# Last stages of a spectral mixer as 64- and 32-row matmul tiles, eight per product

## The chip, the cores and the metric

The kernel runs on one core of one Trainium2 chip. The metric is the device time of one execution in microseconds (us). TensorE (PE) multiplies matrices and loads weights (PEld); VectorE (DVE), ScalarE (ACT) and GpSimd (POOL) compute elementwise; DMAs are issued from the queues of SyncE (SP), ACT and POOL. Results of PE lie in PSUM, eight banks; everything else on the chip lies in SBUF.

## What is computed

With x of shape (1, 2048, 640), the kernel mixes two long convolutions with a gate per row:

```
g = sigmoid((x * gate_w).sum(-1, keepdims=True))
# a: K[d, l] = 2 Re sum_n C[d, n] exp(A[d, n] dt[d] l);
#    y = irfft(rfft(x^T, 4096) * rfft(K, 4096))[:2048];  a = y^T + x * D_skip
# b: irfft2(rfft2(x) * (w_r + i w_i))
out = g * a + (1 - g) * b
```

## The kernel before

Everything is 32-bit floating point. The transforms of length 4096 are done in stages, each a set of small matmuls. Columns (640 of them) are handled as four blocks c of 160. Rows are l = 64 b + a with b below 32 and a below 64.

- `phase_a`, first half: `stage1` (L328) and `stage2` (L340) transform x and store it to DRAM as u_d; at its end four copies (L441) put the gate sums of the rows into `T.gate`, 16 columns of 128 partitions.
- `phase_a`, second half: the part b. `front` loads a slice (ue, L475; ww, L478), `channels`, `filt`, `back1` transform and filter, and `back2` (L559) does the inverse and stores each 128-row result s3 to DRAM as s3e_d by one DMA (L570, L572), from SP for the first six slices, from POOL for the last three.
- `phase_p` and `phase_b`, merged with it: the kernel K of the convolution; y (L679, L680) on POOL feeds the matmuls p_k (L693).
- `phase_c` and `phase_d`: the transform of K in `first`, and block by block the product with u_d and the way back. This last stage is where the change lies.

`phase_d` handles, for each block c, five groups of pairs of frequencies. `fronts` (L784) loads us, does `stage2` into PSUM (p_s2, L348), and on DVE and POOL the complex product (ma, mb, t2; L795 to L801). `backs` (L804) multiplies by `T.w3` into PSUM (p_i2, L814), copies to s3 on ACT (L816, L818), and ACT's queue stores s3 to DRAM as s3_d (L823, and L820 for the single last pair, whose rows overwrite rows of group 8's store). `load_c` (L856) reads s3_d back as t3, with frequency on the partitions, by SP (once by ACT); `load_e` (L852) reads s3e_d as t3e. The last stages then are:

- `last_e` (L868): pieces of three, three and two columns a; `halved` (L157) multiplies t3e by `T.e3e` as two tiles of 128 rows and 64 columns; DVE multiplies by 1 - g into oe (L876).
- `last_c` (L881): the same pieces, from t3 with `T.e3`, two tiles of 128 rows and 64 columns (L893); DVE multiplies by g into ot (L898) and POOL adds oe (L899). For the last block DVE does both in one instruction per column (L896), 16 in all. Output rows go out by DMA (L901, L904, L954).

`T.e3` and `T.e3e` hold the 32-column matrix of the last step in blocks with zeros elsewhere, so that one matmul of 128 rows does two (or four) blocks of the contraction. Each 32-bit matmul shows as two records in the trace, each with a weight load.

PSUM in `phase_d`: the pool `c_ps` of three tiles of two banks for p_s1, p_s2 and p_i2, and the pool `d_ps` of two tiles of one bank for the last stages. A new tile waits until the tile that had its place has been read.

The order of the work: `merge` (L163) draws from several generators by the costs that they yield and their weights. In each group, `mains` (fronts of this group, backs of one or more groups before), `last_e` or `last_c` for the block before, and two steps of `first` for the next block go side by side. `last_e` of block c runs beside groups 1 and 2 (2 and 3 for c = 0), `last_c` of block c - 1 beside groups 3 and 4 for c = 1 and 2. `last_c` of blocks 2 and 3 comes at the end. `behind` only keeps an order on one engine. The engines are strict queues: what stands behind a waiting instruction waits too.

Of the kernel before, what the change touches and what calls it, by code (L numbers as in the profile page):

```python
# [9 lines left out]
F32 = mybir.dt.float32  # L10
# [40 lines left out]
def _tables():  # L51
# [14 lines left out]
    e3 = np.zeros((64, 2, 2, 32))  # L66
    for j in range(2):
        e3[:, j, j, :] = kr

    e3e = np.zeros((32, 4, 4, 32))  # L70
    for r in range(4):
        e3e[:, r, JR[r], :] = kr[32:64]
    one = np.tile(np.eye(32), (4, 1))
    c1 = np.concatenate([
        e1[0], e1[1], e3.reshape(4, 32, 64).swapaxes(0, 1).reshape(128, 64), e3e.reshape(128, 128), np.eye(128), one,
# [16 lines left out]
    w3 = np.swapaxes(w3, 0, 1).reshape(128, NP * 128)  # L92
# [37 lines left out]
    return {"t_c1": f(c1), "t_w2": f(w2), "t_w3": f(w3), "t_td": f(td),  # L130
# [17 lines left out]
def _lay_back(y):  # L148
    y = y.reshape(4, 2, 2, 32, 16, 160)
    return np.ascontiguousarray(y.transpose(3, 2, 1, 4, 0, 5).reshape(1, L, D))  # L150
# [4 lines left out]


def halved(nc, out, w, x):  # L157

    for i in (0, 64):
        nc.tensor.matmul(out[i:i + 64], w[:, i:i + 64], x, start=True, stop=True)  # L160
# [23 lines left out]
def body(tc, A, out):  # L184
    nc = tc.nc
    T = Ctx()
    with ExitStack() as top:
        dram = top.enter_context(tc.tile_pool(name="dram", bufs=1, space=DRAM))
        T.u_d = dram.tile([4, 128, 17, 2, 160], F32, name="u_d")
        T.s3e_d = dram.tile([4, 32, 64, 160], F32, name="s3e_d")  # L190
        T.s3_d = dram.tile([4, 64, 64, 160], F32, name="s3_d")
# [12 lines left out]

        T.e1 = [take(128), take(128)]
        T.e3, T.e3e, T.id, T.one = take(64), take(128), take(128), take(32)
# [146 lines left out]
def phase_a(tc, A, T):  # L353
# [3 lines left out]
    with ExitStack() as ctx:  # L357
# [82 lines left out]
        for r, x in enumerate((slice(31, 15, -1), slice(32, 48), slice(15, None, -1), slice(48, 64))):  # L440
            V.tensor_copy(T.gate[32 * r:32 * r + 32, 0, :], p[32 * r:32 * r + 32, x])  # L441


    with ExitStack() as ctx:
# [16 lines left out]
        w3v = A["t_w3"].rearrange("p (k m) -> p k m", m=128)  # L461
# [8 lines left out]
        def front(pr, st):  # L470
            nl = st.nl = 128 if pr < 8 else 64
            st.w3 = w3p.tile([128, 2, 128], F32, tag="w3", name="w3")
            nc.sync.dma_start(st.w3[:, 0:nl // 64, :], w3v[:, 16 + 2 * pr:16 + 2 * pr + nl // 64, :])
# [85 lines left out]
        def back2(st, pr, j):  # L559
# [9 lines left out]
            if kk < 16:  # L569
                dma(T.s3e_d[:, 2 * kk:2 * kk + 2].rearrange("c k a d -> (k a) c d"), s3.rearrange("p (c d) -> p c d", c=4))  # L570
            else:
                dma(T.s3e_d[:, 1].rearrange("c a d -> a c d"), s3[0:64].rearrange("p (c d) -> p c d", c=4))  # L572
# [193 lines left out]
def phase_d(tc, A, T, ctx, out):  # L766
# [9 lines left out]
    ps = ctx.enter_context(tc.tile_pool(name="c_ps", reuse_waits="tile", bufs=3, space=PSUM))  # L776
    pd = ctx.enter_context(tc.tile_pool(name="d_ps", reuse_waits="tile", bufs=2, space=PSUM))
# [26 lines left out]
    def backs(c, g0, gn, st):  # L804
# [4 lines left out]
        for h in range(0, np_, 4):  # L809
# [9 lines left out]
            if k0 == 32:  # L819
                nc.scalar.dma_start(T.s3_d[c, 33], s3[0:64, 0, :])  # L820
            elif h or (c, g0) == (3, 12):
                x = h if (c, g0) == (3, 12) else 0
                T.sd = nc.scalar.dma_start(T.s3_d[c, 2 * (k0 + x):2 * (k0 + h) + 8].rearrange("(x k) a d -> (k a) x d", k=2), s3[:, x:h + 4, :])  # L823
# [16 lines left out]
    def gate(i, a, n):  # L840
        return T.gate[:, i, a:a + n].unsqueeze(2).broadcast_to([128, n, 160])
# [10 lines left out]
    def load_e(c):  # L852
        t3es[c] = dk.tile([128, 16, 160], F32, tag="t3e", name="t3e")
        nc.sync.dma_start(t3es[c][:, :, :], T.s3e_d[c].rearrange("k (r a) d -> (k r) a d", r=4))

    def load_c(c, p, n, parts=1, eng=nc.sync):  # L856
# [5 lines left out]
        w = 16 // parts  # L862
        for y in range(p // 16, (p + n) // 16):
            src = T.s3_d[c, 16 * y:16 * y + 16].rearrange("k (j x a) d -> (k j) x a d", x=2, j=2)
            for a in range(0, 16, w):
                T.ld = eng.dma_start(t3s[c][y::4, :, a:a + w], src[:, :, a:a + w])

    def last_e(c, a):  # L868

        oe = oes[c, a] = o4.tile([128, AG, 160], F32, tag="oe", name="oe")  # L870
        for i in range(0, AG, 3):
            n = min(3, AG - i)
            p = pd.tile([128, 3, 160], F32, tag="pd", name="p_e")
            with behind(T.mm):
                halved(nc, p[:, 0:n], T.e3e, t3es[c][:, a + i:a + i + n])
            V.tensor_tensor(out=oe[:, i:i + n], in0=p[:, 0:n], in1=gate(1, a + i, n), op=ALU.mult)  # L876
            yield 0.8
# [3 lines left out]
    def last_c(c, a):  # L881
# [6 lines left out]
        for i in range(0, AG, 3):  # L888
            n = min(3, AG - i)
            p = pd.tile([128, 3, 160], F32, tag="pd", name="p_c")  # L890
            with behind(T.mm):
                for x in range(2):
                    P.matmul(p[64 * x:64 * x + 64, 0:n], T.e3, t3[:, x, a + i:a + i + n], start=True, stop=True)  # L893
            if c == 3:
                for j in range(n):
                    V.scalar_tensor_tensor(out=ot[:, i + j], in0=p[:, j], scalar=T.gate[:, 0, a + i + j:a + i + j + 1], in1=oe[:, i + j], op0=ALU.mult, op1=ALU.add)  # L896
            else:
                V.tensor_tensor(out=ot[:, i:i + n], in0=p[:, 0:n], in1=gate(0, a + i, n), op=ALU.mult)  # L898
                (V if c == 2 and a and n < 3 else G).tensor_tensor(out=ot[:, i:i + n], in0=ot[:, i:i + n], in1=oe[:, i:i + n], op=ALU.add)  # L899
            if c < 2 and i + n == AG:  # L900
                G.dma_start(out[c, :, a:a + AG], ot[:, :, :])  # L901
            elif c == 3 and i + n > (5 if a else 6):
                x = i if a and i > 3 else 0
                nc.sync.dma_start(out[c, :, a + x:a + i + n], ot[:, x:i + n])  # L904
            yield 0.8
# [72 lines left out]
```

## Time and profile before

| | |
|---|---|
| time, median of 3 runs | 609.3 us |
| lowest and highest | 607.72 and 2746.93 us |
| the profiled execution: its time | 608.74 us |
| its span in the profile | 607.0 us |
| mean granted TensorE clock | 0.966 |
| HBM | 60.91 MB read, 39.98 MB written |

The median stands 0.6 us above the profiled execution. In rows of instruction groups, "out<-in" names the tile written and those read (buffer numbers left out; a tile goes by a shortened name, so t3 appears as t, s3_d as s_d, e3 as c), and "128*64 128x480" is a matmul on 128 rows and 64 columns of the array, over 480 elements. "idle before <-releaser" is how long the engine sat idle and what ended it.

### The profile page before, as it was taken

To read this page: it belongs to the slowest core of one execution; us is meant where nothing else is said; L and a number is where in the kernel's file an instruction comes from. 1 tells how busy PE (TensorE), PEld (TensorE's weight loads), DVE (VectorE), ACT (ScalarE), POOL (GpSimd) and SP (SyncE) were. 2 spreads that over 40 slices of the span, in tenths; PEclk is the share of its full clock that TensorE was granted. 3 is DMA by queue.
4 is the path that set the end of the run, shared out by engine and by line. 5 is a ranking of instruction groups with operands and counts; after the bars stand their busy time and mean duration, and the time that the engine had idled before them with its cause. 6 is when DMAs were issued, how large, how long until landed. Compare 5 with 4: busy or idle time off the path is not lost.

```text
span 607.0 us, 16654 instructions
## 1 busy us (share of the span) xinstructions
PE 535.8 (88%) x7084; PEld 405.6 (67%) x7084; DVE 500.2 (82%) x748; ACT 364.8 (60%) x659; POOL 267.0 (44%) x246
## 2 busy tenths in 40 slices
PE   9688979989968989989798999898989999999874
PEld 7576657766656657676566676565878877787631
DVE  5971597598899989999999899979399796987974
ACT  4556775576846876888589888799723332231210
POOL 4931252053525344454326335416254347547441
PEclk9899989989989996998899999999999999999998
DMA  8787204245612320332250233006685989889776
GB/s 341 293 288 268 79 5 151 69 154 181 239 43 67 97 87 13 108 118 109 67 151 12 75 97 110 24 28 200 224 346 184 356 273 299 291 271 310 225 231 239
DMA packets 48083, 101.98 MB, mean 168 GB/s; under 512 B 3316, under 2 KB 32776, under 8 KB 46248
## 3 DMA queue, kind: packets, MB, share of 16 engines
q1 hardware_dynamic: 24888, 67.74, 32.3%
q10 hardware_dynamic: 20080, 22.52, 11.9%
q0 software_dynamic: 3040, 10.65, 5.3%
q8 instruction: 56, 0.92, 0.6%
q14 instruction: 19, 0.16, 0.1%
HBM read 60.91 MB, written 39.98 MB: 166 GB/s over the span
## 4 chain that ended last, share of the span: by engine, by line
PE 51%; DVE 27%; ACT 9%; DMA 8%; issue 4%; POOL 1%; ACTq 0%; DVEq 0%; POOLq 0%; SPq 0%
PE p_eo L551 8%; PE p_s L348 8%; PE p_s L335 6%; PE p_e L638 5%; PE p_k L693 4%; PE p_i L814 4%; PE p_p L649 3%; DVE q L652 3%; PE p_d L518 2%; DVE t L801 2%; PE p_i L565 2%; PE p_t L502 2%; DVE ma L795 2%; PE p_c L893 2%; PE p_d L519 2%
## 5 line engine op out<-in xcount | busy, mean ns | idle before, releaser
L679 POOL TENSOR_TENSOR y<-e,sc 128x512 f32<-128x512 f32 x40 | 56.7, 1418 | 131.0 <-ACT sc L665 60.3
L348 PE MATMUL p_s<-t,w 128*64 128x160 f32 x1056 | 92.4, 314 | 10.2 <-ACT ut L382 5.1
L348 PEld LDWEIGHTS p_s<-t,w 128*64 128x64 f32 x1056 | 76.5, 139 | 21.4 <-ACT ut L382 6.0
L640 ACT ACTIVATE e<-p_e 128x512 f32<-128x512 f32 x120 | 68.6, 602 | 22.7 <-PE p_e L638 20.4
L551 PE MATMUL p_eo<-td,pmt 107*128 107x321 f32 x204 | 69.0, 459 | 3.9 <-ACT pmt L505 3.9
L693 PE MATMUL p_k<-x,y 128*32 128x64 f32 x2560 | 63.6, 229 | 9.8 <-DVE x L677 2.9
L693 PEld LDWEIGHTS p_k<-x,y 128*32 128x32 f32 x2560 | 46.1, 113 | 38.0 <-issue 29.4
L652 DVE SCALAR_TENSOR_TENSOR q<-q,p_p 128x512 f32<-128x512 f32 x80 | 53.4, 681 | 13.5 <-ACT q L651 11.8
L336 ACT COPY t<-p_s 128x512 f32<-128x512 f32 x40 | 24.6, 623 | 65.2 <-PE p_s L335 41.8
L638 PE MATMUL p_e<-rm,par 128*128 128x512 f32 x120 | 58.7, 519 | 3.4 <-ACT e L640 2.8
L680 POOL TENSOR_TENSOR y<-e,sc 128x512 f32<-128x512 f32 x40 | 54.5, 1362 | 6.5 <-ACT sc L666 6.5
L800 POOL TENSOR_TENSOR t<-ma 64x320 f32<-64x320 f32 x32 | 28.0, 875 | 61.4 <-DVE ma L795 51.8
L551 PEld LDWEIGHTS p_eo<-td,pmt 107*128 107x128 f32 x204 | 38.4, 198 | 19.6 <-ACT pmt L505 6.9
L677 DVE TENSOR_TENSOR x<-e,cx 128x1024 f32<-128x1024 f32 x40 | 48.6, 1214 | 2.2 <-ACT cx L668 2.2
L651 ACT ACTIVATE q<-p_p 128x512 f32<-128x512 f32 x80 | 46.5, 592 | 4.2 <-PE p_p L649 3.8
L649 PE MATMUL p_p<-rp,par 128*128 128x512 f32 x80 | 43.5, 548 | 4.5 <-DVE q L652 4.5
L814 PE MATMUL p_i<-t,w 128*64 128x160 f32 x528 | 42.7, 300 | 4.4 <-POOL t L801 3.4
L335 PE MATMUL p_s<-c,kt 128*64 128x128 f32 x640 | 43.0, 274 | 3.9 <-DVE mb L796 2.0
L335 PEld LDWEIGHTS p_s<-c,kt 128*64 128x64 f32 x640 | 38.0, 136 | 12.6 <-issue 7.7
L816 ACT COPY s<-p_i 128x640 f32<-128x640 f32 x32 | 21.8, 694 | 40.0 <-PE p_i L814 30.4
L335 PE MATMUL p_s<-c,u 128*64 128x128 f32 x640 | 41.5, 278 | 2.5 <-ACT ut L382 2.5
L795 DVE TENSOR_TENSOR ma<-p_s,us 128x640 f32<-128x640 f32 (+1 forms) x36 | 28.2, 784 | 18.8 <-PE p_s L348 11.5
(153 smaller groups left out, 1181.5 us busy)
## 6 DMA issues: line engine op xcount, KB each, us to landing
u_d<-ut SPq DMA_DIRECT2D x32, 320.0 KB, 2.6
us<-u_d ACTq DMA_DIRECT2D x16, 640.0 KB, 6.0
s_d<-s ACTq DMA_DIRECT2D x15, 640.0 KB, 8.3
t<-s_d SPq DMA_DIRECT2D x14, 640.0 KB, 5.9
ww<-in_w_l SPq DMA_DIRECT2D x8, 642.0 KB, 4.0
ue<-u_d SPq DMA_DIRECT2D x8, 640.0 KB, 4.4
k_d<-kt SPq DMA_DIRECT2D x4, 1280.0 KB, 7.6
kt<-k_d SPq DMA_DIRECT2D x8, 640.0 KB, 5.9
```

The lines of the kernel that those rows point to most:

```text
L335: nc.tensor.matmul(p[64 * ri:64 * ri + 64, j, :], src(i + j), e1[ri], start=True, stop=True)
L348: ins = nc.tensor.matmul(p[64 * j:64 * j + 64, i, 160 * ri:160 * ri + 160], w2[:, x, 64 * ri:64 * ri + 64], t1[:, x // 2 if x < 32 else K0 ...
L551: P.matmul(p[:, :E], st.pmt[:DC, c, w, j, :], tv[:DC, w, c, :], start=c == 0, stop=c == 2)
L638: P.matmul(p[:, :], pars[t], rm[:, c:c + 512], start=True, stop=True)
L640: st.exp = S.activation(ef[:, c:c + 512], p[:, :], AF.Exp)
L649: P.matmul(p[:, :], pars[t], rp[:, c:c + 512], start=True, stop=True)
L652: V.scalar_tensor_tensor(out=qf[:, c:c + 512], in0=qf[:, c:c + 512], scalar=MAGIC, in1=p[:, :], op0=ALU.subtract, op1=ALU.subtract)
L677: V.tensor_tensor(out=x[:, 0].rearrange("p d (h j) -> p d h j", h=2), in0=e[:, :, 0:64].rearrange("p d (h j) -> p d h j", h=2), in1=cx.uns ...
L679: G.tensor_tensor(out=y[:, 1], in0=e[:, :, 64:96], in1=sc[:, 0], op=ALU.mult)
L680: G.tensor_tensor(out=y[:, 0], in0=e[:, :, 64:96], in1=sc[:, 1], op=ALU.mult)
L693: P.matmul(st.pb[32 * r:32 * r + 32, o, :], y[:, ri, 4 * qq + JR[r], :], x[:, ri, 4 * qq + JR[r], :], start=t % 2 + qq + 1 - ri == 0, stop ...
L814: T.mm = P.matmul(p[x:x + 64, i // 2, 160 * (i % 2):160 * (i % 2) + 160], T.w3[:, k0 + h + i, x:x + 64], t2[:, h + i, :], start=True, stop ...
```

## The change

The last stages do a product in eight matmuls: four blocks s of output partitions (32 columns each) times two halves j of the contraction rows. For `last_c` each matmul has 64 rows, for `last_e` 32, and each covers two columns a (320 elements). One product thus gives four columns, in two PSUM banks, one for each j; a group of eight columns is two products instead of three pieces. `T.e3` and `T.e3e` lose their zeros and shrink to 32 columns. The products share the pool `c_ps`, now four tiles of two banks; `d_ps` is gone.

To have the rows in the order that this needs, the columns of `T.w3` are permuted (and a second table `t_w3e` serves part b), s3_d and s3e_d have new shapes, each store of s3_d goes out as two DMAs over every second partition, and each store of s3e_d as four over every fourth. Loads of t3 that were cut in two by columns are cut by the halves x. The gate is written by 16 copies instead of four, and the output's row order changes with it. The core of the diff:

```
-        for r, x in enumerate((slice(31, 15, -1), slice(32, 48), slice(15, None, -1), slice(48, 64))):
-            V.tensor_copy(T.gate[32 * r:32 * r + 32, 0, :], p[32 * r:32 * r + 32, x])
+        for r in range(4):
+            o = slice(32 * r, 32 * r + 32)
+            g = T.gate[o, 0, :].rearrange("p (x j v) -> p x j v", x=2, j=2)
+            for x in range(2):
+                i = 16 * x + 4 * r
+                V.tensor_copy(g[:, x, 0], p[o, 31 - i:(27 - i if i < 28 else None):-1])
+                V.tensor_copy(g[:, x, 1], p[o, 32 + i:36 + i])
...
-            if kk < 16:
-                dma(T.s3e_d[:, 2 * kk:2 * kk + 2].rearrange("c k a d -> (k a) c d"), s3.rearrange("p (c d) -> p c d", c=4))
+            sv = s3.rearrange("p (c d) -> p c d", c=4)
+            for r in range(4):
+                if kk < 16:
+                    dma(T.s3e_d[:, r, 2 * kk:2 * kk + 2].rearrange("c k a d -> (k a) c d"), sv[r::4])
...
-    ps = ctx.enter_context(tc.tile_pool(name="c_ps", reuse_waits="tile", bufs=3, space=PSUM))
-    pd = ctx.enter_context(tc.tile_pool(name="d_ps", reuse_waits="tile", bufs=2, space=PSUM))
+    ps = ctx.enter_context(tc.tile_pool(name="c_ps", reuse_waits="tile", bufs=4, space=PSUM))
...
+            for j in range(2):
+                if k0 == 32:
+                    nc.scalar.dma_start(T.s3_d[c, 2, j, 1], s3[j:64:2, 0, :])
+                elif h or (c, g0) == (3, 12):
+                    x = h if (c, g0) == (3, 12) else 0
+                    T.sd = nc.scalar.dma_start(T.s3_d[c, g0 // 4, j, 2 * x:2 * h + 8].rearrange("(x k) a d -> (k a) x d", k=2), s3[j::2, x:h + 4, :])
...
+    def product(w, t, x, v, rows):
+
+        p = ps.tile([128, 2, 512], F32, tag="ps", name="p_l")
+        with behind(T.mm):
+            for s in range(4):
+                for j in range(2):
+                    r = slice(64 * j + rows[0], 64 * j + rows[1])
+                    P.matmul(p[32 * s:32 * s + 32, j, 0:320], w[r, :], t[r, 4 * s + v:4 * s + v + 2, :], start=True, stop=True)
+        return p[:, :, 0:320].rearrange("p j (v d) -> p j v d", v=2)
...
-        for i in range(0, AG, 3):
-            n = min(3, AG - i)
-            p = pd.tile([128, 3, 160], F32, tag="pd", name="p_e")
-            with behind(T.mm):
-                halved(nc, p[:, 0:n], T.e3e, t3es[c][:, a + i:a + i + n])
-            V.tensor_tensor(out=oe[:, i:i + n], in0=p[:, 0:n], in1=gate(1, a + i, n), op=ALU.mult)
+        x = a // AG
+        for v in (0, 2):
+            p = product(T.e3e, t3es[c], x, v, (32 * x, 32 * x + 32))
+            V.tensor_tensor(out=four(oe, v), in0=p, in1=gate(1, a, v), op=ALU.mult)
...
+            p = product(T.e3, t3[:, x], x, v, (0, 64))
...
+                V.tensor_tensor(out=four(ot, v), in0=p, in1=gate(0, a, v), op=ALU.mult)
+                (V if c == 2 and a and v else G).tensor_tensor(out=four(ot, v), in0=four(ot, v), in1=four(oe, v), op=ALU.add)
```

The last block's output goes out as one DMA of 640 KB for the first eight columns of each partition and two of 320 KB for the other eight; before, it was 640, 480 and 160 KB.

More of the change, by code (lines that the diff above doesn't have):

```diff
@@ L148, in _lay_back @@
 def _lay_back(y):
-    y = y.reshape(4, 2, 2, 32, 16, 160)
-    return np.ascontiguousarray(y.transpose(3, 2, 1, 4, 0, 5).reshape(1, L, D))
+    y = y.reshape(4, 4, 32, 2, 2, 4, 160)
+    return np.ascontiguousarray(y.transpose(2, 4, 3, 1, 5, 0, 6).reshape(1, L, D))
 class Ctx:
     pass
-def halved(nc, out, w, x):
-    for i in (0, 64):
-        nc.tensor.matmul(out[i:i + 64], w[:, i:i + 64], x, start=True, stop=True)
 def merge(*streams):
@@ L887, in last_c @@
             ot = up.tile([128, 4, 2, 160], F32, tag="us", name="ot").rearrange("p x y d -> p (x y) d")
[L888 to L893, printed above, removed]
+        x = a // AG
+        for v in (0, 2):
+            p = product(T.e3, t3[:, x], x, v, (0, 64))
             if c == 3:
[L895 to L900 removed]
+                for j in range(2):
+                    for i in range(v, v + 2):
+                        o = 4 * j + i
+                        V.scalar_tensor_tensor(out=ot[:, o], in0=p[:, j, i - v], scalar=T.gate[:, 0, a + o:a + o + 1], in1=oe[:, o], op0=ALU.mult, op1=ALU.add)
+            else:
+                V.tensor_tensor(out=four(ot, v), in0=p, in1=gate(0, a, v), op=ALU.mult)
+                (V if c == 2 and a and v else G).tensor_tensor(out=four(ot, v), in0=four(ot, v), in1=four(oe, v), op=ALU.add)
+            if c < 2 and v:
                 G.dma_start(out[c, :, a:a + AG], ot[:, :, :])
[L902 to L905, printed above, removed]
+            elif c == 3 and (v or a):
+                o = out[c, :, a:a + AG]
+                if a:
+                    nc.sync.dma_start(four(o, v), four(ot, v))
+                else:
+                    nc.sync.dma_start(o, ot[:, :, :])
+            yield 1.2
         if c == 2:
```

52 lines of the change are left out of this document (23 added, 29 removed).

## The prediction

> **What bounds the kernel now.** I read the busy shares first, then the busy times of the last stretch, then the chain of waits through it, then the rows of the work that changes. Of the page:
>
> ```profile
> span 607.0 us, 16654 instructions
> PE 535.8 (88%) x7084; PEld 405.6 (67%) x7084; DVE 500.2 (82%) x748; ACT 364.8 (60%) x659; POOL 267.0 (44%) x246
> ```
>
> PE leads, but the average covers stages with different limits. The changed stages lie after 440 us. Busy times there (length, PE, PEld, DVE, ACT, POOL, then clock, DMA share, GB/s):
>
> ```profile
> 440.00:577.80 137.80, 126.24 (x1594) 104.21 (x1592) 118.47 (x168) 39.45 (x63) 73.39 (x80) 1.00 0.86 284
> 577.80:595.80 18.00, 10.18 (x92) 5.57 (x89) 11.04 (x15) 1.71 (x4) 9.72 (x10) 1.00 0.73 217
> 595.80:607.00 11.20, 6.65 (x24) 1.87 (x24) 5.13 (x16) 0.00 (x0) 0.00 (x0) 0.83 0.65 256
> 480.00:500.00 20.00, 18.61 (x248) 15.30 (x246) 19.34 (x27) 5.40 (x10) 9.64 (x11) 1.00 0.88 287
> 500.00:520.00 20.00, 19.05 (x237) 15.99 (x234) 14.07 (x22) 6.51 (x11) 13.72 (x16) 1.00 0.97 319
> ```
>
> PE, DVE and DMA are all near full: PE 92% and DMA 86% of the 137.8 us. In 480 to 500 DVE has 0.66 us of slack in 20, PE 1.39; in 500 to 520 DVE has 5.93 and PE 0.95. So a faster PE is worth much in the second kind of window and little in the first. The chain from 440 us on (start, length, what):
>
> ```profile
> by line: PE p_i L814 13.8%; PE p_s L348 12.8%; DVE t L801 8.5%; DVE ma L795 7.8%; PE p_c L893 7.5%; DVE mb L796 7.4%; DMA s_d<-s 7.0%; PE p_e L160 6.0%; PE p_s L335 5.8%; issue 5.6%; DVE t L800 4.5%; DVE oe L876 3.6%; DMA t<-s_d 2.2%; ACT s
> 463.24 0.81 PE p_e L160 x4
> 466.00 0.54 PE p_e L160 x4
> 489.57 0.87 PE p_s L335 x16
> 511.45 0.41 ACTq L823
> 511.90 0.60 ACT t L336
> 577.86 8.84 DMA s_d<-s
> 586.79 0.48 ACTq L820
> 587.37 0.54 ACTq L823
> 588.68 2.91 DMA s_d<-s
> 591.65 3.75 DMA t<-s_d
> 595.81 4.06 PE p_c L893 x12
> 599.89 1.04 PE p_c L893 x4
> 602.07 0.77 PE p_c L893 x4
> ```
>
> The last-stage matmuls (p_e, p_c) hold 13.5% of 167 us, 22.5 us, of which 5.87 us are the last three rows: 16.6 us lie in the middle. From 577.86 to 595.4 the end hangs on ACT's stores and on DMA landings, not on PE.
>
> **The change, part by part.** *PE.* A piece of three columns (480 elements) takes 0.81 us, one of two (320) 0.54, with two tiles side by side. So four columns cost 1.08. A product of the new form does four columns with eight matmuls of 320 elements: 0.54 if all eight run at once, 1.08 if only four do, plus the change of tile shape, which the old form did not have (all its neighbours were 64 wide). The nearest rows are those of p_k, four tiles of 32 columns between 64-wide work:
>
> ```profile
> 432.68 1.97 PE L335 MATMUL p_s<-c,kt 128*64 128x128 f32 x32
> 434.57 1.10 PE L693 MATMUL p_k<-x,y 128*32 128x64 f32 x64
> 434.57 0.94 PEld L693 LDWEIGHTS p_k<-x,y 128*32 128x32 f32 x64 [0.17 <-issue]
> 435.61 1.97 PE L335 MATMUL p_s<-c,kt 128*64 128x128 f32 x32
> L693 PEld LDWEIGHTS p_k<-x,y 128*32 128x32 f32 x2560 | 46.1, 113 | 38.0 <-issue 29.4
> ```
>
> Sixteen p_s records take 0.87, so 32 should start the next group after 1.74; it came after 1.89. The 64 p_k records took 1.04. Two at once, 64 elements each, would need 64 x 64 / (4 x 320) x 0.54 = 1.73; four at once 0.86. So four at once is shown, with 0.18 left over, and a change in and out costs 0.15 + 0.18, about 0.3. For eight, no row has two row groups at work; from two to four tiles the gain was whole, so I take 0.54, a product of 0.84, 0.24 less than 1.08, and keep 1.38 as the other end. Sixteen products for p_e and eight for p_c lie before 577.8: PE loses 5.8 us of work. On the chain that is at most 16.6 x 0.24/1.08 = 3.7 us and at least none, where DVE is late next. p_c's part (7.5% less the 5.87, 6.6 us) stands where DVE has slack and counts whole, 1.5; p_e's (10 us) mostly where it has not, and I count a third of its 2.2, 0.7. Together 2.2 us.
>
> One thing could undo all this. If the loads of a row group's four tiles had to take turns with their matmuls, a product would take eight loads of 0.113 and eight passes of 0.27 (half of 0.54), 3.1 us. The p_k rows speak against it: 64 loads, 7.2 us in all and on the same 128 rows, went through in 0.94 us, among their matmuls. That they must take turns is what the Trainium skill states, page "TensorE: Matmul & The Clock Gate", Part 3, on what overlaps and what doesn't: a weight load overlaps a running matmul only where the row group differs. The trace here disagrees.
>
> *DVE.* The evacuation of p_e (that of p_c has the same shapes), and the row whose shape the new ones have:
>
> ```profile
> L876 DVE TENSOR_TENSOR oe<-p_e,gate x24: 481/658/659, 456.6 to 576.2; 128x480 f32<-128x480 f32 x16, 128x320 f32<-128x320 f32 x8
> L795 DVE TENSOR_TENSOR ma<-p_s,us x36: 473/825/827, 439.7 to 582.2; 128x640 f32<-128x640 f32 x32, 64x320 f32<-64x320 f32 x4
> ```
>
> For p_e, 16 x 0.66 + 8 x 0.49 = 14.5 us become 16 x 0.825 = 13.2; oe has 3.6% of the chain, 6.0 us, so 0.5. For the p_c before 577.8, half as many, 7.2 become 6.6, mostly beside PE: 0.1. The two banks of p_e and p_c are merged with the others: eight before, eight after, so I cost that at nothing; the cover is that a product's bank is free after one 0.825 us multiply, and if it goes PE waits behind DVE's ma (0.825) and what follows that.
>
> *ACT's queue.* Each store of s_d becomes two:
>
> ```profile
> L823 ACTq DMA_DIRECT2D s_d<-s x17: 366/377/1037, 459.9 to 588.7; - x17
> L820 ACTq DMA_DIRECT2D s_d<-s x4: 468/474/482, 487.5 to 586.8; - x4
> ```
>
> That is 17 x 0.38 + 4 x 0.47 = 8.3 us more issuing. Most is hidden, ACT being busy 39.45 of 137.8 us. At 511.45 the issue stands in the chain right ahead of a copy; the code comes to the same place once more, one block later: 2 x 0.4 = 0.8. At the end, L823 at 587.37 and the one at 588.68 double: 0.54 + 0.37 = 0.9. L820 at 586.79 waits for the store of 577.86, whose rows it overwrites; its first half can go while the second half of that store lands, so 0.2 (bounds 0 and 0.48). The bytes and the 640-byte runs are unchanged, so I leave landing times as they are. The loads of t and of t3e keep their runs too.
>
> *The end.* The final DVE instructions:
>
> ```profile
> 597.23 0.97 DVE L896 SCALAR_TENSOR_TENSOR ot<-p_c,gate,oe 128x160 f32<-128x160 f32 x3 [4.11 <-PE p_c L893]
> 598.83 1.74 DVE L896 SCALAR_TENSOR_TENSOR ot<-p_c,gate,oe 128x160 f32<-128x160 f32 x5 [0.63 <-PE p_c L893]
> 600.96 2.59 DVE L896 SCALAR_TENSOR_TENSOR ot<-p_c,gate,oe 128x160 f32<-128x160 f32 x8 [0.39 <-PE p_c L893]
> ```
>
> DVE works 5.3 us of 6.32, with gaps of 0.63 and 0.39 for PE, whose clock is low: the first three pieces take 4.06 where 0.81 + 0.81 + 0.54 = 2.16 would do, 1.9 times. A product of eight at once then takes 0.54 x 1.9 = 1.0, less than DVE's four instructions (1.3), so both gaps go: -1.0. Only-four would give 2.0 a product and PE sets the pace. The last store is 320 KB instead of 160: at the 256 GB/s of the last window 160 KB are 0.6, of which I take 0.4.
>
> *Earlier stages.* The stores of s3e become four each; the five on POOL and the twelve on SP:
>
> ```profile
> 411.25 1.59 POOL L570 DMA_DIRECT2D s3e_d<-s  x2 [0.48 <-ACT s L566]
> 412.86 1.30 POOL L679 TENSOR_TENSOR y<-e,sc 128x512 f32<-128x512 f32 x1
> 425.61 3.71 PE L335 MATMUL p_s<-c,kt 128*64 128x128 f32 x64 [1.31 <-DMA kt<-k_d]
> SPq L570 <- ACT s L566: 85.0, 9, 21.0
> L441 DVE COPY gate<-p_g x4: 154/170/179, 152.9 to 153.5; 32x16 f32<-32x16 f32 x4
> 153.65 0.99 DVE fo L482
> 154.67 4.58 DMA ue<-u_d
> ```
>
> POOL issues 15 more of 0.8, 12 us. Six of them stand ahead of the y at 412.86, which moves 4.8 us; p_k waits for it, then the p_i and copies behind. PE's wait of 1.31 for kt at 425.61 takes up some: 0.5 (0 to 2). SP issues 36 more, at ACT's 0.38 about 14 us, among 85 us in which its queue waits for the copies ahead of these stores: nothing, and up to 1 us if the loads of ue and ww behind them come late. The gate becomes 16 copies instead of 4, 12 x 0.17 = 2.0 us on DVE. They stand before fo L482, which starts the load of ue on the whole chain, so little hides them: 1.6 (0 to 2).
>
> *Sum:* -2.2 - 0.6 + 0.8 + 1.1 - 1.0 + 0.4 + 0.5 + 1.6 = +0.6 us on the profiled execution. That one took 608.74 us (span 607.0), 0.6 under the 609.3 median; 608.74 + 0.6 = 609.3.
>
> **The rivals.** *PE's whole gain comes through.* If the p_e and p_c of the chain shrink without DVE taking over, 3.7 replaces 2.2; if POOL, the gate and ACT's two issues stay hidden (-2.9): 609.3 - 1.5 - 2.9 = 604.9. For it: PE 92% busy in the stretch. Against: DVE at 19.34 of 20. Even all 5.8 us gives no more than 602.8.
>
> *Two row groups do not run together.* Then a product takes 1.38, 0.30 more than before: 24 x 0.30 = 7.2 us of PE, between 4.7 (chain's share) and 7.2 of time instead of -2.2, and at the end 2.0 instead of 1.3 for each of the last three products, +2.2. That gives 609.3 + 9.1 to 11.6, 618 to 621. It decides as soon as a product costs over 1.08. For it: no row shows two row groups. Against: the whole gain from two tiles to four.
>
> *Weight loads take turns:* 24 x (3.1 + 0.3 - 1.08) = 56 us of PE, nearly all of it time: 662. The p_k rows speak against it.
>
> *The queues stop it:* a store's second half waits at the head of ACT's queue, behind it the copies that free PSUM. If that costs 0.5 us for each of the 21 stores, 10 us, 619. For it: landings of 8.84 us. Against: ACT is idle over two thirds.
>
> **How the numbers follow.** Forecast (605.5 to 614) 0.64; whole gain 0.12; row groups in turn 0.13; queues 0.09; weight loads 0.02. I predict 609.3. The whole gain and most of the two slower cases belong in the range: 603 to 620. It leaves out the top of those two, the weight loads and what I overlook, about 0.14. By 2%, about what a measurement of this kernel can tell from no change, the bounds are 597.1 and 621.5. Faster: no case reaches it, 0.02 for what I overlook. Slower: a third of the row groups and queues, whose upper ends lie at that bound, 0.07, the weight loads 0.02 and 0.03 overlooked: 0.12. Same: 0.86.
>
> **What would show it.** Products of about 0.54 us of starts with 0.3 around them show the tiles right; 1.1 the row groups in turn. DVE's last sixteen without gaps, a second store at 0.4 behind each first, y late by about 5 us near 412, and 16 gate copies before fo L482 show the rest. The forecast is wrong if PE's share of the chain falls and no other grows, or if ACT or PE newly waits for a landing in the middle stretch.

## The result and the profile after

| | before | after |
|---|---|---|
| median | 607.79 us (22 runs) | 614.84 us (22 runs, 608.06 to 622.23) |
| ratio after to before | | 1.0076, 95% interval [1.0046, 1.0105] |
| profiled execution: time, span, mean clock | 608.74, 607.0, 0.966 | 608.06, 606.3, 0.961 |
| median of its runs' mean granted clocks | 0.967 (17 runs) | 0.946 (14 runs) |

The change makes the kernel 0.8% slower: less than the 2% of the classes, more than its interval. The time lies in the range, but the forecast was no change. The profiled execution of after is the shortest of its 22, so its span shows none of the loss; what it does show is what the new parts cost. (Ratios, and the clocks given for runs, leave out a kernel's runs that lie over 1.5% above its fastest, 8 of the 22 here; with them the medians differ by 1.2%.) The 17 runs of before with a clock are those beside the first experiments.

The page of after, its span and busy shares:

```profile
span 606.3 us, 17403 instructions
PE 521.8 (86%) x7404; PEld 397.4 (66%) x7404; DVE 498.4 (82%) x746; ACT 365.4 (60%) x659; POOL 272.1 (45%) x255
```

Busy times of after in the stretches that the prediction showed for before (length, PE, PEld, DVE, ACT, POOL, clock, DMA share, GB/s), and of five short ones:

```profile
440.00:577.80 137.80, 121.50 (x1824) 98.96 (x1822) 116.15 (x155) 39.71 (x63) 73.35 (x76) 0.96 0.84 285
577.80:595.80 18.00, 7.06 (x124) 4.66 (x120) 10.92 (x13) 1.82 (x4) 8.79 (x7) 0.92 0.65 201
595.80:607.00 11.20, 3.97 (x64) 1.70 (x64) 4.76 (x16) 0.00 (x0) 0.00 (x0) 0.65 0.63 247
...
446.00:449.60 3.60, 1.35 (x16) 1.07 (x16) 3.54 (x5) 0.08 (x1) 2.23 (x3) 1.00 1.00 420
449.60:456.40 6.80, 3.94 (x40) 2.83 (x42) 5.85 (x8) 0.61 (x1) 3.33 (x4) 0.50 0.13 45
456.40:460.00 3.60, 3.60 (x62) 2.85 (x60) 2.61 (x4) 1.32 (x2) 1.67 (x2) 0.99 0.66 192
558.90:562.30 3.40, 1.69 (x32) 1.09 (x24) 3.34 (x5) 0.29 (x1) 1.38 (x2) 0.99 0.63 203
562.30:565.70 3.40, 3.40 (x28) 2.98 (x26) 2.69 (x4) 1.25 (x2) 1.47 (x2) 0.50 0.37 106
```

PE has 4.7 us less to do in the middle stretch and DVE 2.3 us. But in this stretch the clock, 1.00 throughout in before, stands at one half twice, for 6.8 and 3.4 us. The first time has its reason in the timeline of PE (start, length, operation, idle before and what ended it). Before:

```profile
449.93 1.07 PE L335 MATMUL p_s<-c,kt 128*64 128x128 f32 x16
451.02 1.36 PE L348 MATMUL p_s<-t,w 128*64 128x160 f32 x16
452.24 0.43 PE L335 MATMUL p_s<-c,kt 128*64 128x128 f32 x2
452.60 1.83 PE L160 MATMUL p_e<-t3e,c 128*64 128x480 f32 x8
```

After:

```profile
446.81 1.35 PE L339 MATMUL p_s<-t,w 128*64 128x160 f32 x16 [1.37 <-DVE mb L793]
452.46 1.32 PE L877 MATMUL p_l<-t3e,c 32*32 32x320 f32 x16 [4.31 <-DMA t3e<-s3e_d]
453.71 1.98 PE L326 MATMUL p_s<-c,kt 128*64 128x128 f32 x16
455.48 1.76 PE L339 MATMUL p_s<-t,w 128*64 128x160 f32 x16
...
459.13 0.77 PE L877 MATMUL p_l<-t3e,c 32*32 32x320 f32 x16
459.82 1.31 PE L811 MATMUL p_i<-t,w 128*64 128x160 f32 x16
```

The load of t3e lands at about 452.5 us in both kernels. In before, PE did a p_s from kt and a p_s from t in that time; in after the first product stands ahead of them in PE's queue, PE waits 4.31 us, and what follows runs at half the clock: 1.32 us for the product, 1.98 for a p_s that takes 1.04 to 1.09 elsewhere. Later products cost 0.69 us from start to start (459.13 to 459.82). The Trainium skill, page "TensorE: Matmul & The Clock Gate", Part 1, says that the clock halves after an idle window of about 3.4 us. The trace agrees in the length, with halves of 6.8 and 3.4 us. It does not agree in the condition: PE was busy for 1.35 of the 3.60 us ahead of the first half and for 1.69 of the 3.40 ahead of the second, where no wait was longer than 1.71 us.

In all 20 traces kept here, stretches of one clock last multiples of 3.41 us. Counted in such steps, the clock went from full to half 231 times, after steps in which PE was busy for at most 63% (median 40%); it stayed full after every step above that, and came back from half only after steps of at least 83%. ("Busy" is the profile's, in which the ends of matmuls are modelled.)

The issues of the stores in after (ns, shortest/median/longest; first and last start):

```profile
L821 ACTq DMA_DIRECT2D s_d<-s x34: 587/648/2592, 461.9 to 589.3; - x34
```

```profile
L818 ACTq DMA_DIRECT2D s_d<-s x8: 496/580/627, 489.4 to 586.6; - x8
```

A half does not cost what a whole store did (0.377 us) but 0.648, and up to 2.6. The 34 took 29.4 us together. From the waits of after from 440 us on (in total, times, longest), two on landings that were 1.3 and 0.2 us in before:

```profile
ACT s L813 <- DMA s_d<-s: 6.4, 2, 4.7
...
PE p_l L877 <- DMA t3e<-s3e_d: 4.3, 1, 4.3
```

The end of the chain of after, to be read against the rows from 586.79 us on in the prediction:

```profile
586.61 0.63 ACTq L818
587.23 0.04 issue
587.27 1.29 ACTq L821
588.56 0.04 issue
588.60 0.63 ACTq L821
589.23 0.03 issue
589.26 2.33 DMA s_d<-s
...
591.72 4.67 DMA t<-s_d
596.39 0.14 issue
596.53 1.39 PE p_l L877 x16
597.92 0.02 issue
597.94 3.01 DVE ot L905 x10
```

The last 16 DVE instructions now have no gap (timeline of DVE):

```profile
597.94 4.76 DVE L905 SCALAR_TENSOR_TENSOR ot<-p_l,gate,oe 128x160 f32<-128x160 f32 x16 [6.55 <-PE p_l L877]
```

### The profile page after: what moved, and what is told of

Same layout as the page of the kernel before. It is cut to its first block, busy times and chain, and to the rows that moved or that the text cites. A ratio compares the mean times of both kernels' runs of the same rounds, so it can differ in the third digit from the quotient of the medians.

```text
span 606.3 us, 17403 instructions
## 1 busy us (share of the span) xinstructions
PE 521.8 (86%) x7404; PEld 397.4 (66%) x7404; DVE 498.4 (82%) x746; ACT 365.4 (60%) x659; POOL 272.1 (45%) x255
## 5 line engine op out<-in xcount | busy, mean ns | idle before, releaser
L547 PE MATMUL p_eo<-td,pmt 107*128 107x321 f32 x204 | 67.5, 452 | 3.9 <-ACT pmt L501 3.9
L691 PE MATMUL p_k<-x,y 128*32 128x64 f32 x2560 | 61.3, 224 | 8.6 <-DVE x L675 3.3
L691 PEld LDWEIGHTS p_k<-x,y 128*32 128x32 f32 x2560 | 44.4, 110 | 35.5 <-issue 28.5
L811 PEld LDWEIGHTS p_i<-t,w 128*64 128x64 f32 x528 | 35.6, 139 | 16.5 <-issue 10.7
```

The source lines that it names most:

```text
L547: P.matmul(p[:, :E], st.pmt[:DC, c, w, j, :], tv[:DC, w, c, :], start=c == 0, stop=c == 2)
L691: P.matmul(st.pb[32 * r:32 * r + 32, o, :], y[:, ri, 4 * qq + JR[r], :], x[:, ri, 4 * qq + JR[r], :], start=t % 2 + qq + 1 - ri == 0, stop ...
L811: T.mm = P.matmul(p[x:x + 64, i // 2, 160 * (i % 2):160 * (i % 2) + 160], T.w3[:, k0 + h + i, x:x + 64], t2[:, h + i, :], start=True, stop ...
```

## The experiments

Two theories at first. C: PE is less busy, so its clock is granted lower. Q: the loss comes from the doubled store DMAs and from ACT's queue. Four of the kernels compute another output; their expectations say so.

**Is it the lighter PE, or the stores?** The changed kernel again, unedited:

> The changed kernel once more, to see how its time goes with the granted clock. Theory C (the clock): the faster products leave TensorE less busy in the middle stretch, so the clock is halved there for some 3.4 us at a time, in some executions more often; then the time falls on a line with the mean granted clock, some 3 to 4 us longer for each 0.01 of clock, from about 607 us at 0.96 to 617 at 0.93, and the kernel before stays near 608 at a higher clock. Theory Q (the queues: the split stores take 0.6 us or more to issue instead of 0.38 and delay ScalarE's copies): the time is longer by 4 to 7 us at the same clock, and the profile shows ScalarE late in the middle. Either way about 4 to 6 us slower than before.

Measured: 617.06 us, 1.0128 [1.0068, 1.0189]. The loss is there again, at a median clock of 0.935. With each product's eight matmuls issued twice:

```diff
-            for s in range(4):
-                for j in range(2):
+            for s, j in [(s, j) for _ in range(2) for s in range(4) for j in range(2)]:
```

> The changed kernel with the eight matmuls of every product issued twice, so that TensorE is about as busy with the last stages as in the kernel before; the second set writes the same values. Theory C: the clock stays up in the middle (mean 0.95 or more in nearly all executions) and the time comes down to within 2 us of the kernel before, 606 to 610, though there is 17 us more matmul work. Theory Q: the work added to a TensorE that is 88% busy makes it slower than the changed kernel, 616 to 622.

Measured: 623.22 us, 1.0244 [1.0195, 1.0292], clock of its runs 0.947. More PE work brings back a part of the clock at most (0.947 beside the 0.935 of the unedited kernel, where before had 0.967) and none of the time: theory C in this form falls. The split of the s3 stores alone, on the old tiles:

```diff
-  T.sd = nc.scalar.dma_start(T.s3_d[c, ...]..., s3[:, x:h + 4, :])
+  for j in range(2):
+      T.sd = nc.scalar.dma_start(T.s3_d[c, ...]...[j], s3[j::2, x:h + 4, :])
```

> The kernel before with each store of s3 to s3_d cut into two DMAs over every second partition, as in the change, and nothing else. Theory Q: slower than before by 3 to 6 us, with issues of 0.6 us and more on ScalarE's queue. Theory C: the matmuls are as before, the clock stays, and only the issues on the chain and at the end count, 1 to 2 us.

Measured: 620.28 us, 1.0190 [1.0144, 1.0236]. The split of the s3e stores alone:

```diff
+            for r in range(4):
+                dma(T.s3e_d[...][r], sv[r::4])
```

> The kernel before with each store of s3e cut into four DMAs over every fourth partition, as in the change, and nothing else. Theory Q: slower by 1 to 3 us, through GpSimd late with y near 412 us and through SyncE's loads of ue and ww behind the stores. Theory C: within 1 us of before.

Measured: 610.04 us, 1.0029 [0.9997, 1.0061]. On the old tiles, then, the split of s3 alone costs 11 us, more than the whole change; the quarters of s3e cost little or nothing.

**What about a split store is dear?** First, partitions that lie apart. Both w3 tables permuted so that the halves lie on 64 neighbouring partitions:

```diff
-    w3 = w3.reshape(NP, 128, 2, 2, 32).transpose(1, 0, 2, 4, 3)...
+    w3 = w3.reshape(NP, 128, 2, 2, 32).transpose(1, 0, 3, 2, 4)...
-    s3[j::2, x:h + 4, :]
+    s3[64 * j:64 * j + 64, x:h + 4, :]
```

> The changed kernel with the columns of both w3 tables put in such an order that each half (and each quarter of s3e) lies on neighbouring partitions (0 to 63, 64 to 127) and not on every second (or fourth) one; the number of DMAs, their bytes and their rows in DRAM are as in the changed kernel. Theory P (what makes a half dear is its partitions lying apart): the issue of a half falls from the 0.587 us (median) of the changed kernel towards the 0.37 us of the whole store of before, and the time to 607 to 611 us. Theory N (it is the number of DMAs and issues, wherever their partitions lie): issue stays at 0.47 to 0.6 us and the time at 613 to 618 us.

Measured: 618.24 us, 1.0088 [1.0041, 1.0134], and the issue is as dear as in the changed kernel, 0.648 us (the expectation's 0.587 was the shortest of that row, not its median). The row of the store:

```profile
L821 ACTq DMA_DIRECT2D s_d<-s x34: 582/648/2172, 473.8 to 602.6; - x34
```

It is not the stride of the partitions that makes the issue dear. Then the queue, with every second half issued by SP:

```diff
-    T.sd = nc.scalar.dma_start(...)
+    T.sd = (nc.sync if j else nc.scalar).dma_start(...)
```

> The changed kernel with each second half of an s3 store issued by SP, so that ACT issues as many stores as before the change, while the number of DMAs is the same as in the changed kernel. Theory A (the loss comes from ACT's queue: an issue of 0.6 us and more stands ahead of ACT's next copies, which the second product waits for): ACT is as free as before, the new tiles keep their gain, 603 to 608 us. Theory N (the loss is the doubled number of DMAs, whichever queue issues them): 613 to 619 us. A rival of its own: SP's queue then waits for ACT's copy ahead of each half and holds up its loads behind that; then over 617 us, with SP's waits on ACT in the profile.

Measured: 612.12 us, 1.0039 [1.0000, 1.0079], between the two expectations. The long issues are gone from ACT, while in the profiled execution its copies wait more for landings (two views, issues and waits). That execution took 617.77 us, near the top of its twelve, so how much of the wait is usual is not shown:

```profile
L821 SPq DMA_DIRECT2D s_d<-s x17: 579/609/1140, 475.0 to 598.1; - x17
L821 ACTq DMA_DIRECT2D s_d<-s x17: 591/596/673, 475.0 to 598.1; - x17
```

```profile
ACT s L813 <- DMA s_d<-s: 14.4, 4, 5.0
```

A store that stays whole, with the loads of t3 cut in two instead:

```diff
+    T.sd = nc.scalar.dma_start(T.s3_d[c, g0 // 4, x:h + 4].rearrange("x j k a d -> (j k a) x d"), s3[:, x:h + 4, :])
+    for j in range(2):
+        T.ld = eng.dma_start(t3s[c][64 * j + y:64 * j + 64:4, x:x + w], T.s3_d[c, y, :, j]...)
```

> The changed kernel with s3 stored whole again, one DMA from all 128 partitions: DRAM holds the rows as (x, j, k, a), so that a block's store is one pattern, and the loads of t3 go by j instead, two DMAs by SP (or, for the last piece but one, by ACT) where there was one. ACT then issues 17 whole stores and 4 small ones as before the change, and the tiles of the last stages stay new. Theories A and N alike: 602 to 608 us, no slower than the kernel before, since the split was all the loss and the products cost 0.69 us for 0.96 to 1.08 us before. If instead the new tiles or the gate cost time by themselves, 611 to 616 us stays.

Measured: 651.63 us, 1.0724 [1.0669, 1.0780], a clear miss. From its chain:

```profile
505.14 11.42 DMA t<-s_d
541.22 11.68 DMA s_d<-s
554.22 13.12 DMA t<-s_d
578.23 11.67 DMA s_d<-s
```

A load of 320 KB onto 16 partitions, read as 8 by 2 rows, takes 11 to 13 us, where one of 640 KB onto 32 partitions took 5.2 (median in after). The Trainium skill, page "DMA: Bandwidth & Descriptors", section "Why a DMA increments its semaphore by 16 and not by 1", says that a DMA uses the largest number of engines up to 16 that divides the slowest dimensions of both its patterns, here 8. If both loads of a pair share the same 8, they would take twice 5.2, 10.4 us, an estimate near the times; but the 16 engines together were busy for 0.89 and 0.90 of the two stretches of these loads (from 505.2 and 554.3 us), so the run does not show that cause. The whole stores beside these loads took 11.7 us too, so the run says nothing about whole stores by themselves. Then ACT's time by itself, one idle copy of 0.62 us behind each wide store of the kernel before, and two:

```diff
+                S.copy(xa[:, :, :], T.w2[:, 0:4, :])
```

> The kernel before, with one copy of 128x512 on ACT (reads a table, writes a tile that nothing reads) behind each of the 18 wide s3 stores: about 0.62 us each by the 623 ns of the same shape in the first product's copies, 11 us of ACT in all, and no DMA more. The output is not touched. Theory A (ACT's time at that place is the cost): about as dear as the split store alone, 616 to 621 us. Theory N (the number of DMAs, their landings and the waits between them): 607 to 612 us.

Measured: 609.05 us, 1.0035 [0.9997, 1.0073]. (The wide stores, and so the copies, are 17, not 18.)

> The kernel before with two idle copies on ACT behind each of the 18 wide s3 stores, 1.25 us a block and some 22 us in all, no DMA more; nothing of the computation is touched. The two halves take about 1.3 us a block together where the whole store took 0.38 us, so that this is a little more of ACT's time than the split takes. Theory A in its plain form (any time of ACT at this place costs): one copy cost a ratio of 1.0035, two cost as much as the split alone, 1.015 to 1.025. If ACT's time is not it, but the DMAs themselves: 1.003 to 1.008.

Measured: 612.13 us, 1.0084 [1.0046, 1.0121], just above what was expected if ACT's time is not it. And the split on the old tiles with every second half on SP (the edit of the split alone and that of SP together):

> The kernel before with its old tiles, each s3 store split into two halves as in the run of the split alone (ratio 1.019), but the second half issued by SP. The number of DMAs is that of the run of the split alone, ACT's issues are as many as before. Theory A (the cost comes by ACT's queue): ratio 1.000 to 1.005, 608 to 612 us. Theory N (number of DMAs): ratio 1.015 to 1.02, 617 to 621 us.

Measured: 617.74 us, 1.0166 [1.0133, 1.0199], where theory N had it. But the two losses lie at different places of the traces, so the number of transfers is not shown to be the cause. From the first ma product to the 28th before takes 114.6 us, the split alone 122.4, the split with SP 110.8; from there to the end of the span they take 52.7, 55.0 and 66.6 us. With SP's help the loss of the middle is gone, which speaks for ACT's queue there. Another stands at the end, where SP's halves wait for ACT's copies (waits of SP's queue from 440 us on) with SP's loads behind them:

```profile
SPq L824 <- ACT s L816: 54.1, 11, 8.5
```

Whether this wait is what costs was not tried apart. So idle time of ACT is worth some 0.8%; what else the split on the old tiles costs, by its queues, by the number of transfers or by their shape, stays open. Nor is it quite the split of the change: on the old tiles a half writes every second row of 640 bytes in DRAM, in the changed kernel neighbouring rows.

**The order on PE.** The timeline above suggested a third theory, O: the first product stands too early.

```diff
         x = a // AG
+        if (c, a) == (0, 0):
+            yield 0.6
```

> The changed kernel with its first product taken one step later: PE's order then has one more first product (sixteen matmuls of p_s from kt) and one more second product ahead of the first eight matmuls on t3e, as the kernel before had. All else is as in the changed kernel. Theory O (the change moved its first product ahead of work that PE could do while the load of t3e was under way, so PE stands still for 4.3 us at 448 us, and runs at half the clock after it): the wait falls under 2 us, the step from the ninth to the tenth ma product falls from the 5.8 us of the changed kernel to 2 to 3 us, and the time falls by 3 to 6 us, to 609 to 612 us. Theory N (all the loss is the doubled store DMAs): 614 to 618 us, as the changed kernel.

Measured: 613.20 us, 1.0041 [1.0000, 1.0082]. The wait and the half clock are gone, as PE's timeline and the window of this kernel show:

```profile
451.91 1.07 PE L326 MATMUL p_s<-c,kt 128*64 128x128 f32 x16
452.78 1.34 PE L339 MATMUL p_s<-t,w 128*64 128x160 f32 x16
456.36 0.77 PE L877 MATMUL p_l<-t3e,c 32*32 32x320 f32 x16 [2.24 <-DVE ma L792]
```

```profile
449.00:461.00 12.00, 7.20 (x113) 5.92 (x110) 11.75 (x17) 2.14 (x4) 6.89 (x8) 1.00 0.62 235
```

The wait of 2.24 us is a little over the 2 expected. The step that the expectation calls ninth to tenth, from the fifth ma product to the sixth, is 3.2 us (455.50 to 458.73), as in before. But the intervals of this ratio and of the changed kernel's overlap: the wait is explained, its worth, some 0.4% by the ratios, is not settled. With SP for the second halves as well:

> Both edits together: the first product one step later, and the second half of every s3 store issued by SP. If the loss is the sum of the two (the order at 448 us, and the halves on ACT's queue), this is the changed kernel with both taken out and with its cheaper products kept: 603 to 607 us, below the kernel before. If the halves cost by their number alone, 608 to 613 us.

Measured: 612.13 us, 1.0041 [1.0004, 1.0078], the second of the two. The gains do not add up.

**Front or back?** The new front (16 gate copies and the quarters of s3e) also changes the order of the work behind it: from the gate copies on, PE, DVE, ACT, POOL and SP get their instructions in another order than before, through most of a stage up to 430 us that the diff hardly touches. In before DVE's fo of one slice came in two parts, L481 at 219.81 and L482 at 248.40; in after it comes at once:

```profile
219.81 0.82 DVE L481 TENSOR_TENSOR fo<-ue 128x640 f32<-128x640 f32 x1
248.40 1.78 DVE L482 TENSOR_TENSOR fo<-ue 128x640 f32<-128x640 f32 x1
```

```profile
245.56 0.82 DVE L477 TENSOR_TENSOR fo<-ue 128x640 f32<-128x640 f32 x1
246.29 1.89 DVE L478 TENSOR_TENSOR fo<-ue 128x640 f32<-128x640 f32 x1
```

This example comes with the quarters: in the run of the quarters alone this fo comes at once too (244.45 and 245.18 us), in that of the gate copies alone, below, in two parts (220.36 and 246.45). The quarters alone measured 0.3%, an interval that includes no change and a clock over 0.966; so another order of the front need not be dear.

The two ends of the change were crossed. The new front with the old back:

> The front of the change with the back of the kernel before: the sixteen gate copies and the s3e stores by quarters as in the changed kernel, the last stages' tiles and the whole s3 stores as before (the gate's columns then stand in an order that the old tiles do not use, so that the output is another). The order of the work on PE is the changed kernel's up to its first product. Theory F (the front is what costs the clock and the time): ratio 1.005 to 1.01, mean clock about 0.945. Theory K (the back costs): ratio 1.000 to 1.004, clock 0.96 and more.

Measured: 612.68 us, 1.0080 [1.0051, 1.0108]; clock 0.952. (Its quarters write every fourth row of 640 bytes in DRAM, those of the changed kernel neighbouring rows.) The old front with the new back:

> The other half: the new tiles, the halves of s3 and the loads of the changed kernel, with the gate's four copies and the whole s3e stores of the kernel before (the gate and s3e then hold their values in the old order, so that the output is another; bytes and shapes of what is read later are the same). Up to the first product the order on PE is that of the kernel before. Theory F: ratio 0.997 to 1.003 and a clock of 0.955 to 0.965. Theory K: ratio 1.007 to 1.012 and a clock of 0.94.

Measured: 611.76 us, 1.0043 [1.0006, 1.0079]; clock 0.947. The gate copies alone, on the kernel before:

> The kernel before with the sixteen gate copies alone (the output is another, since the old tiles use the old order of columns). By their own time they add 0.8 us on DVE at 152 us; but they change which work stands first in the stage behind them. Theory F with the gate as its cause: ratio 1.004 to 1.01 and a clock of 0.945. If they cost only their time or less: 1.000 to 1.003, clock 0.96 and more.

Measured: 609.62 us, 1.0033 [0.9996, 1.0071]; clock 0.957, between the two. The old front, the new back and the later product:

> The run of the new back with the old front, and its first product one step later as well (gate and s3e hold their values in the old order, so that the output is another). If the early product is all that the back costs, the new tiles, dearer stores and all, are left with their gain: ratio 0.993 to 1.000 and a clock of 0.955 and more. If the back costs by its stores or its tiles as well: 1.002 to 1.006.

Measured: 609.65 us, 1.0034 [0.9996, 1.0072]; clock 0.955, in the second of its ranges: with the old front the later product gained 0.1% by the ratios, not the whole cost of the back. Theories F and K were half right: front and back cost something each, and their sum, 1.2%, lies between the 0.8 and 1.3% that the changed kernel showed.

The profiled executions, divided at the start of the first ma product, add this (one execution each). From there to the end of the span before takes 167.3 us, the changed kernel 167.7 and with the later product 163.2; the new back on the old front 170.2 and with the later product 167.9; the split on the old tiles 177.4, with and without SP. Ahead of it, the seven kernels whose front is that of before took 439.6 to 445.4 us, the nine with the new front 437.5 to 449.8. So one execution does not show what a front costs; only the medians do. Two attempts at a better kernel, with the later product and the gate's order made by TensorE, so that DVE copies once or four times:

```diff
+                P.matmul(pg[o, x, 0], T.one, lr[:, 31 - i:(27 - i if i < 28 else None):-1], start=True, stop=True)
+                P.matmul(pg[o, x, 1], T.one, lr[:, 32 + i:36 + i], start=True, stop=True)
+        V.tensor_copy(T.gate[:, 0, :], p[:, 0:16])
```

> The changed kernel with its first product one step later, and with the gate's order made by TensorE: sixteen small matmuls of four columns each write the sums in the new order, and DVE copies them once (128x16) where it copied sixteen times. The halves of s3 stay. If the front's cost comes from the copies, this is the run of the later product without it: 603 to 608 us, below the kernel before; if it comes from elsewhere, 610 to 614 us. The order of the front is again another one here, so that a result between the two would say only that this order matters.

Measured: 614.83 us, 1.0070 [1.0028, 1.0112].

```diff
+            P.matmul(p[o, 0:32], T.one, lr[:, 31::-1], start=True, stop=True)
+            P.matmul(p[o, 32:64], T.one, lr[:, 32:64], start=True, stop=True)
+            V.tensor_copy(T.gate[o, 0, :].rearrange("p (x j v) -> p x j v", x=2, j=2), p[o, :].rearrange("p (j x r v) -> p r x j v", j=2, x=2, r=4)[:, r])
```

> The changed kernel with its first product later and the gate in four copies: eight matmuls write the sums with the first 32 columns turned round, and DVE copies 32 rows with all 16 columns at a time. DVE's order up to the second stage is nearly that of the run of the s3e quarters alone. If the front's cost is the copies' and the order that they brought: 603 to 609 us, ratio 0.993 to 1.001. If it is the order of the front in general, which is again another here: 1.002 to 1.008.

Measured: 614.31 us, 1.0112 [1.0058, 1.0166]. Fewer copies do not help; each version brings its own order of the front, and whether that order is the reason is not shown. No kernel tried here beats the one before.

## Why the prediction was wrong

**The step that failed** is the sum, in both of its halves. Its terms for the front, "+ 0.5 + 1.6" for s3e and the gate, make 2.1 us; the new front with the old back measured 0.8%, 4.9 us (3.1 to 6.6 by its interval). Its terms for the back, "-2.2 - 0.6 + 0.8 + 1.1 - 1.0 + 0.4", make a gain of 1.5 us; the new back with the old front measured a loss of 0.43%, 2.6 us (0.4 to 4.8). Neither half has a term for a change of order or of clock: every term is a duration at the clock and in the order of the profile of before, and neither stayed. In the back, one such step is "I cost that at nothing": PE then waited 4.31 us for a landing and ran at half the clock for 6.8, worth 0.1 to 0.4% by the runs with the later product, whose intervals do not settle it. Another is "8.3 us more issuing": it was 25 us, and how much of that reached the time is not shown. In the front the step between the new order and the lower clock is not known.

At an equal clock the changed kernel is the faster one. A straight line through time against mean clock, over the runs of before beside all experiments (99, clocks 0.956 to 0.976), gives 611.3 us at 0.956; one over the changed kernel's runs, the first result's and the repeat's (19, clocks 0.932 to 0.961), gives 609.3 there. So at that clock the work is about 2 us shorter, not 0.6 longer. But the median clocks are 0.966 and 0.945, and the lines fall by 360 and 320 us per 1.00 of clock, so these 0.021 are 6.7 to 7.6 us; less the 2 that is 4.7 to 5.6, and the ratio of 1.0076 is 4.6 on 608 us. This is bookkeeping, not a cause: a PE that does little in a step of 3.41 us is granted less in the next, and a PE that is granted less is late. Causes were tried one by one above: front and back each carry part of it.

Point by point:

- *Products.* "I take 0.54, a product of 0.84": a product costs 0.69, well under the 1.08 of only four tiles at once. If all eight run at once in 0.54, the change of shape costs 0.15 and not 0.3. From the tenth ma product to the last, after takes 104.9 us (476.73 to 581.66), before 108.0 (474.27 to 582.23). The mechanism was right, and the gain of 3.0 us there is a little over the 2.2 + 0.6 given to PE and DVE. But from the first to the tenth after takes 38.1 us for 34.6 and loses it again. The row groups in turn (1.38) and the weight loads in turn (3.1) are ruled out.
- *"I cost that at nothing" (shared banks) and "the loads of t and of t3e keep their runs too".* The landing stayed; what stood behind it changed. From the fifth ma product to the sixth before takes 3.2 us (452.64 to 455.87), after 5.8 (451.54 to 457.35). The prediction named the sign of it, "if ACT or PE newly waits for a landing in the middle stretch", but gave it no term. Whether the new costs of the generators or the shared pool put the product first was not tried apart.
- *ACT's queue.* "17 x 0.38 + 4 x 0.47": a half takes 0.648 at the median and up to 2.6, so that 34 wide issues took 29.4 us where 17 took 7.2, and 8 small ones 4.6 where 4 took 1.9: 25 us more, not 8.3. "I leave landing times as they are" did no harm by the medians (8.3 us for a whole store in before, 7.2 for a half in after), but the split alone costs 1.9% on the old tiles, 1.7% when SP shares it, which no term holds. The rival that the queues stop it had the sign, and the middle of the split alone speaks for it; idle time of ACT by itself is worth some 0.8%. Why the new back costs only 0.4% with its split stays open. If the split costs as much there as on the old tiles, the new tiles by themselves win over 1%; that is not shown, since no arrangement was found that has the tiles without the split.
- *The end.* The gaps are gone as forecast; DVE's last stretch is 4.76 us for 6.32. From ACT's first issue there to the last store 2.6 us pass (586.61 to 589.23) for 1.9 (586.79 to 588.68, 0.70 of them a copy), +0.7 for the +1.1 forecast. From the last ma product to the end it is 24.6 us for 24.7; the sum of the terms of this part, +0.5, was 0.6 too dear.
- *s3e and the gate.* The y at 412.86 hardly moved (412.96, and 0.85 us later behind the y before it, not 4.8): the program's order put it between the fours of stores, and PE's wait for kt fell from 1.31 to 0.37 us, so the 0.5 was nothing. The gate copies took 1.57 us for 0.71, +0.9 and not 1.6. What the front costs besides no term held: the gate copies alone measured 0.33%, the quarters alone 0.29%, each with an interval that includes no change, both together 0.8%.

Open: what in the front lowers the clock, what in the back costs once the first product is later, and what the split costs on the old tiles besides ACT's time.

## What to carry to other kernels

A sum of durations holds only for an unchanged order and an unchanged clock: where an edit lets a queue be ordered anew, compare the order of the instructions first, and ask of each operand that is being loaded what will stand behind its wait. On an engine whose clock follows its activity, price a stretch in which it does little at more than its length: here steps of 3.41 us with PE busy for less than some 60% were those that could halve the clock of the next. Split a store only after timing the split by itself: bytes and run lengths did not foretell its cost here.

## What was not expected of the hardware

- Eight matmuls of 64 or 32 rows by 32 columns on 320 elements take 0.69 us, entry and exit included, where two tiles of 64 columns needed 1.08 for the same output.
- A DMA from 64 partitions takes longer to issue than one from 128 with the same rows per partition: 0.648 against 0.377 us (medians), on neighbouring partitions as on every second one, on ACT and (0.609) on SP.
- The clock fell to one half without an idle step of 3.41 us: within a pause of 4.31 us, for 6.8 us, and behind waits of 0.67 and 1.71 us close together, for 3.4. A pause of 2.24 us left it at 1.00.
